# Counting one port for GpSimd and VectorE in the model that writes a fused attention, gated product and expert kernel's order

## The chip, the cores and the metric

The kernel runs on one core of a Trainium2 chip. The metric is the device time of one execution in microseconds (us). Five engines work side by side, each through its own queue and strictly in that queue's order: TensorE (PE; its weight loads are shown apart, as PEld), VectorE (DVE), ScalarE (ACT), GpSimd (POOL) and SyncE (SP), which here only issues DMA transfers. An engine waits for another through semaphores, where the data demand it.

## The reference

Three steps follow one another: attention in chunks with eight memory keys, a gated product, and eight experts whose weights are balanced over all 3072 tokens before they are used.

```python
for c in range(nc):                       # chunks of 32 queries, of 16 + 32 + 8 keys and 8 memory keys
    scores = scale * np.matmul(q_c, k_full.transpose(0, 1, 3, 2))
    a = np.exp(scores - np.max(scores, axis=-1, keepdims=True))
    a = a / (np.sum(a, axis=-1, keepdims=True) + 1e-09)
    out[:, :, c_start:c_end] = np.matmul(a, v_full)
...
x = (x @ w_a) * (x @ w_b) @ w_out         # 3072 x 512, through 1536
...
P = np.exp(x @ w_gate - max)              # 3072 x 8, then scaled over rows and columns 8 times
for e in range(8):
    out += P[:, e:e + 1] * (np.maximum(x @ w1[e], 0.0) @ w2[e])   # 512 -> 1024 -> 512
```

## The kernel before, in words

Every matrix factor is split into a high part (its fp32r rounding, made by ACT) and a low part (the factor less its high part, made by DVE or POOL), and each product is three matmuls.

The first part, up to some 820 us, holds attention and the gated product. Attention goes by 64 groups of 96 queries and four heads: scores on PE (`s_ps`, L401); mask and scale on DVE (`masked`, L410, reading PSUM and one tile in SBUF); the row maximum on DVE (L416); four exponentials on ACT (L419); a tiny addition and a reciprocal of the sums on DVE (`sm`, L425 and L428); the scaling by them on POOL (`norm`, `s_sb`, L431); transposes on PE (`t_ps`, L438), a copy on ACT, the values on PE (`o_ps`, L448), and the high and low part of the result (L456 on ACT, L459 on DVE). The weights of the gated product come in six pieces of 128x512 for each of 24 weight steps. In the first six steps a piece is first turned from 64-bit to 32-bit numbers: L215 on ACT, then `d_clamp` L219, `d_shift` L223, `d_top` L230 and `d_low` L237 on DVE, in the tiles `raw_e` and `raw_m`. In all steps ACT then makes the high part of a piece (L251) and POOL the low one (`w_low`, L255, called a low below). The products are `pab` on PE (12 matmuls a product), `a_sb` on DVE (L549, reads PSUM), `gh` on ACT (L555), its low part `gl` on DVE (L558, two tiles in SBUF), `po` on PE and its sum `acc` on DVE (L573, reads PSUM). From 210 us on DVE and ACT also prepare weights of the experts ahead (tiles `dbuf` and `pbuf`, L271 and L287).

The second part multiplies the experts by a scheme with seven instead of eight block products (`pa`, `px` for the first product, `py`, `pr` for the second). DVE adds, subtracts and splits 128x1024 tiles (`hb`, `xbig`, L271), and `settle` (L928) multiplies by the gate: `hb<-part,pb` with two operands in SBUF, `hb<-pa,pb` with one in PSUM. Until about 1200 us POOL makes the low parts of the experts' weights (`wbig<-raw_e`, 28 of 128x768 and 28 of 128x1024); behind that it has nothing more to do.

The order in each engine's queue is set when the program is built. `Order.add(engine, cost, due, f, *after)` notes an operation, its cost in us, its due number and what it follows. `Order.emit` plays a clock through these costs: whenever an engine is free in the model, it takes the ready operation with the smallest due, and the instructions are written out in that order. There is one `Order` for each part. The model's times go nowhere else: on the chip only the queues' orders and the semaphores are left. In `emit` the engines are visited in the order in which they first occur in the list of operations, DVE ahead of POOL in both parts.

Of the kernel before, what the change touches and what calls it, by code (L numbers as in the profile page):

```python
# [15 lines left out]
ALU = mybir.AluOpType  # L16
# [30 lines left out]
class Order:  # L47

# [10 lines left out]
    def add(self, engine, cost, due, f, *after):  # L59
        self.ops.append((engine, cost, due, f, [x for x in after if x is not None]))  # L60
        return len(self.ops) - 1

    def emit(self):
        follow = [[] for _ in self.ops]
        missing = [len(op[4]) for op in self.ops]
        for x, op in enumerate(self.ops):
            for y in op[4]:
                follow[y].append(x)
        BEGIN, FREE, DONE = range(3)
        ready = {op[0]: [] for op in self.ops}  # L70
        busy = dict.fromkeys(ready, False)

        events = [(0.0, x, BEGIN) for x, m in enumerate(missing) if m == 0]
        heapq.heapify(events)
        begin = [0.0] * len(self.ops)
        left = len(self.ops)
        while events:
            now = events[0][0]
            while events and events[0][0] <= now:
                _, x, what = heapq.heappop(events)  # L80
                engine, cost, due, f, after = self.ops[x]
# [10 lines left out]
            for engine, queue in ready.items():  # L92
                if queue and not busy[engine]:
                    _, x = heapq.heappop(queue)
                    cost, f, store = self.ops[x][1], self.ops[x][3], engine == "ACT" and self.ops[x][1] == 0.1
                    busy[engine] = True
                    f()
                    left -= 1
                    heapq.heappush(events, (now + cost, x, FREE))
                    land = self.land if engine == "SP" or store else 0.0  # L100
                    heapq.heappush(events, (now + cost + land, x, DONE))
        assert left == 0
# [3 lines left out]
def tile_kernel(ctx: ExitStack, tc, qT, kw, vw, w_moe, w_gate, w_ex, out):  # L106
# [166 lines left out]
    def weight_ops(add, w, blocks, sums, due, loaded, before=(), pool=True):  # L273
# [5 lines left out]
        y = add("DVE", 0.42, d, lambda: sub(s1, w22, w21, ALU.add), loaded, *before)  # L279
        y = add("DVE", 0.42, d, lambda: sub(s3, w11, w21), y)  # L280
        y = add("DVE", 0.42, d, lambda: sub(s2, s1, w11), y)
        summed = add("DVE", 0.42, d, lambda: sub(s4, w12, s2), y)
        done = []
        for cost, x, a, n, y in ((0.83, 0, blocks, 3, loaded), (1.05, 3, sums, 4, summed)):
            h, lo = w[:, x:x + n, 0, :], w[:, x:x + n, 1, :]
            a = a[:, :n * Q].rearrange("p (i n) -> p i n", i=n)
            y = add("ACT", cost, d, lambda h=h, a=a: nc.scalar.activation(out=h, in_=a, func=AF.Copy), y, *before)  # L287
            done.append(y)
            if pool:
                done.append(add("POOL", 2.4 * cost, d, lambda h=h, lo=lo, a=a: sub(lo, a, f32(h), engine=nc.gpsimd), y))  # L290
                continue
            for b in range(0, n, 2):
                c = min(b + 2, n)
                done.append(add(
                    "DVE", 0.35 * (c - b), d, lambda h=h[:, b:c], lo=lo[:, b:c], a=a[:, b:c]: sub(lo, a, f32(h)), y))
        return done

    def token_ops(add, sb, due, stage, cs, after, free, ahead=1.0, gate=()):
# [16 lines left out]
        def split(i, src, d, *deps):  # L315
            h, lo = (x[:, i, cs[0]:cs[0] + n].rearrange("p c t -> p (c t)") for x in x7)
            y = add("ACT", 1.05 * k1, d, lambda: nc.scalar.activation(out=h, in_=src, func=AF.Copy), *deps, free[i], *gate)
            return add("DVE", 1.2 * k1, d, lambda: sub(lo, src, f32(h)), y)
# [3 lines left out]
        y1 = add("DVE", 1.2 * k1, due, lambda: sub(n0, b22, b12), in22, in12, *gate)  # L322
        y2 = add("DVE", 1.2 * k1, due, lambda: sub(b12, b12, b11), y1, in11)
        y3 = add("DVE", 1.2 * k1, due, lambda: sub(n1, b22, b12), y2)
# [5 lines left out]
        y4 = add("DVE", 1.2 * k1, due + 0.05, lambda: sub(b11, b21, n1), y3, ready[B11])  # L330
# [6 lines left out]
    with ExitStack() as pa:  # L337
# [53 lines left out]
        def attn_group(x, i, g, qk_loaded, v_loaded, due):  # L391
# [72 lines left out]
            y = add("DVE", 0.07, due, sums, *[add("ACT", 0.39, due, lambda j=j: exps(j), y) for j in range(4)])  # L464
# [62 lines left out]
        def moe_step(x, n, s, k):  # L527
# [63 lines left out]
            for f in range(NF):  # L591
# [13 lines left out]
                z = add("DVE", 0.47, due, lambda f=f: g_low(f), z)  # L605
# [357 lines left out]
    def operands(g):  # L963
# [5 lines left out]
        for k, (q, j) in enumerate(((0, 0), (0, 1), (1, 0), (1, 1))):  # L969
            done = [h_done[g, q, j, i] for i in range(2)]  # L970
            if g < HOLD:
# [3 lines left out]
                    "DVE", 1.2, at - 0.1 + 0.2 * q, lambda src=src, dst=dst, j=j:  # L975
# [10 lines left out]
        def split(p, src, n, *deps):  # L986
# [6 lines left out]
            y = add("DVE", 1.2, d, lambda: sub(lo, src, f32(h)), y)  # L993
# [4 lines left out]
        def summed(o, a, b, n, *deps):  # L998
            return add("DVE", 1.2, at + (n - 2.2) * step, lambda: sub(o, a, b), *deps)
# [247 lines left out]
```

## Time and profile before

| | |
|---|---|
| three runs | 2684.62, 2686.83, 2687.25 us (median 2686.83) |
| the profiled execution | 2686.72 us, of which the span of the instructions is 2684.7 us |
| PE busy in the span | 2620.5 us (98%) |
| DVE busy | 2141.1 us (80%) |
| ACT busy | 1056.2 us (39%) |
| POOL busy | 458.8 us (17%), 270 instructions |

Times inside the profile count from the span's start. Busy time is the time in which an instruction of the engine was running or held at its start; an instruction that is ready but held therefore shows as one that takes long. PE's busy time also holds matmuls that wait in its pipeline, so it says little about a full PE. The chain of waits follows the work that ended last back to the start: each piece of it is a time that nothing else covered.

### The profile page before, as it was taken

Reading aid. Unit: us, or ns where it says so; the run is one execution under the profiler, and the core shown is the slowest. Engines: PE = TensorE matmul, PEld = TensorE weight load, DVE = VectorE, ACT = ScalarE, POOL = GpSimd, SP = SyncE. Lnnn points to the kernel's source line nnn. Section 1 sums busy time; section 2 is a strip of 40 time slices with the busy share of each in tenths; the row PEclk is TensorE's granted clock in tenths of the full one; section 3 lists DMA queues with packets and bytes.
Section 4 is the critical chain, followed back from the end, with each engine's and each line's share of the span. In section 5 each row is a group of like instructions: output and inputs, shape, how many; then the busy total and the mean of one; then the engine's idle time right before and its main releaser. Section 6 shows DMA issues by size and latency. Waiting matters only on the chain.

```text
span 2684.7 us, 36063 instructions
## 1 busy us (share of the span) xinstructions
PE 2620.5 (98%) x13147; PEld 2240.8 (83%) x13147; DVE 2141.1 (80%) x3091; ACT 1056.2 (39%) x1914; POOL 458.8 (17%) x270
## 2 busy tenths in 40 slices
PE   6989999999999999999999999999999999999998
PEld 4879989989997788888887888888888888888887
DVE  8994787787768899989999587777789587777777
ACT  6643554654434433433333332222324322222222
POOL 4433342343311422322220000000000000000000
PEclk8999999999999999999999999999999999999999
DMA  7653677777835666666676766666666766666663
GB/s 231 200 162 113 236 247 269 253 245 277 288 108 181 216 231 235 211 246 217 228 257 204 220 202 199 202 203 191 202 219 212 217 198 205 198 194 203 199 187 112
DMA packets 224079, 565.05 MB, mean 210 GB/s; under 512 B 21232, under 2 KB 41712, under 8 KB 219808
## 3 DMA queue, kind: packets, MB, share of 16 engines
q1 hardware_dynamic: 190112, 445.31, 52.8%
q10 hardware_dynamic: 33792, 117.44, 11.6%
q8 instruction: 105, 1.72, 0.3%
q14 instruction: 70, 0.57, 0.1%
HBM read 423.12 MB, written 139.56 MB: 210 GB/s over the span
## 4 chain that ended last, share of the span: by engine, by line
PE 90%; DVE 7%; issue 1%; POOL 1%; ACT 1%; DMA 0%; SPq 0%; ACTq 0%; POOLq 0%; DVEq 0%
PE py L262 25%; PE pa L262 19%; PE pab L262 14%; PE px L262 14%; PE po L262 7%; PE pr L262 7%; PE s_ps L401 1%; DVE sums L271 1%; DVE xbig L271 1%; PE o_ps L448 1%; PE t_ps L438 1%; PE pl L583 1%; DVE hb L271 1%; POOL s_sb L431 1%; DVE gl L558 1%
## 5 line engine op out<-in xcount | busy, mean ns | idle before, releaser
L262 PE MATMUL py<-xbig,wbig 128*128 128x512 f32 x3168 | 801.7, 390 | 4.8 <-DVE sums L271 2.9
L262 PEld LDWEIGHTS py<-xbig,wbig 128*128 128x128 f32 x3168 | 592.3, 188 | 136.8 <-DVE sums L271 10.5
L992 ACT ACTIVATE xbig<-hb 128x1024 fp32r<-128x1024 f32 x336 | 354.9, 1061 | 671.0 <-PE py L262 471.0
L262 PE MATMUL pa<-xbig,wbig 128*128 128x512 f32 x2304 | 586.4, 390 | 1.9 <-DVE part L271 1.3
L271 DVE TENSOR_TENSOR xbig<-hb,xbig 128x1024 fp32r<-128x1024 f32 x336 | 433.9, 1293 | 106.8 <-ACT xbig L992 106.6
L262 PEld LDWEIGHTS pa<-xbig,wbig 128*128 128x128 f32 x2304 | 431.1, 188 | 92.9 <-DVE part L271 2.5
L271 DVE TENSOR_TENSOR sums<-py,sums 128x512 f32<-128x512 f32 x495 | 339.1, 686 | 156.8 <-PE py L262 152.3
L262 PE MATMUL pab<-xbig,wbig 128*128 128x384 f32 x2304 | 448.2, 343 | 0.7 <-ACT a_sb L546 0.7
L262 PE MATMUL px<-xbig,wbig 128*128 128x512 f32 x1728 | 441.6, 390 | 1.0 <-DVE part L271 0.6
L262 PEld LDWEIGHTS pab<-xbig,wbig 128*128 128x128 f32 x2304 | 410.2, 192 | 6.1 <-ACT a_sb L546 0.9
L262 PEld LDWEIGHTS px<-xbig,wbig 128*128 128x128 f32 x1728 | 322.9, 188 | 68.7 <-DVE part L271 1.4
L271 POOL TENSOR_TENSOR wbig<-raw_e,wbig 128x768 fp32r<-128x768 f32 (+1 forms) x56 | 172.0, 3072 | 447.4 <-ACT wbig L287 367.3
L271 DVE TENSOR_TENSOR hb<-hb,hb 128x1024 f32<-128x1024 f32 x192 | 234.8, 1231 | 1.0
L262 PE MATMUL po<-gh,wbig 128*128 128x384 f32 x768 | 234.0, 346 | 0.0
L914 ACT ACTIVATE part<-pa 128x512 f32<-128x512 f32 x192 | 114.3, 595 | 289.7 <-PE pa L262 288.9
L262 PE MATMUL pr<-xbig,wbig 128*128 128x512 f32 x864 | 217.2, 389 | 0.4 <-DVE sums L271 0.4
L928 DVE SCALAR_TENSOR_TENSOR hb<-part,pb 128x512 f32<-128x512 f32 x276 | 193.6, 705 | 2.8
L262 PEld LDWEIGHTS pr<-xbig,wbig 128*128 128x128 f32 x864 | 162.1, 188 | 34.2 <-DVE sums L271 0.6
L271 DVE TENSOR_TENSOR part<-px,part 128x512 f32<-128x512 f32 x192 | 131.6, 686 | 36.7 <-PE px L262 34.7
L573 DVE TENSOR_TENSOR acc<-po,acc 128x384 f32<-128x384 f32 x160 | 88.3, 552 | 75.2 <-PE po L262 74.6
L262 PEld LDWEIGHTS po<-gh,wbig 128*128 128x128 f32 x768 | 143.4, 190 | 5.8
L255 POOL TENSOR_TENSOR wbig<-raw_e,wbig 128x512 fp32r<-128x512 f32 x96 | 127.5, 1348 | 87.1 <-ACT wbig L251 86.9
(121 smaller groups left out, 2219.3 us busy)
## 6 DMA issues: line engine op xcount, KB each, us to landing
wbig<-wc SPq DMA_DIRECT2D x336, 512.0 KB, 3.8
wbig<-wc SPq DMA_DIRECT2D x476, 256.0 KB, 3.3
wc<-xbig ACTq DMA_DIRECT2D x36, 1792.0 KB, 7.7
wc<-wbig ACTq DMA_DIRECT2D x28, 1792.0 KB, 8.3
raw_e<-w_f SPq DMA_DIRECT2D x72, 256.0 KB, 5.0
raw_e<-in_w_ex SPq DMA_DIRECT2D x28, 512.0 KB, 5.3
pb<-pT SPq DMA_DIRECT2D x23, 512.0 KB, 4.9
dbuf<-in_w_moe SPq DMA_DIRECT2D x18, 512.0 KB, 4.6
```

Of the source, the lines that this page charges most:

```text
L255: nc.gpsimd.tensor_tensor(out=wl, in0=raw(part), in1=f32(wh), op=ALU.subtract)
L262: nc.tensor.matmul(out=out, lhsT=a, rhs=b, start=first and i + j == 0, stop=last and i == n - 1 and j == 2, skip_group_check=skip,)
L271: (engine or nc.vector).tensor_tensor(out=out, in0=a, in1=b, op=op)
L401: nc.tensor.matmul(out=s_banks[:TQ, j % 2, 2 * g + j // 2, :], lhsT=qps[i % NQ][a:a + 64, (h0 + j) // 2, :], rhs=kts[i][a:a + 64, (h0 + j) ...
L431: nc.gpsimd.tensor_tensor(out=r["s"], in0=r["s"], in1=r["sm"][:, :, None].to_broadcast([TQ, 4, TK]), op=ALU.mult)
L438: nc.tensor.transpose(r["t_ps"][:, j, :], r["s"][:, j, :], ident[:TQ, :TQ])
L448: nc.tensor.matmul(out=r["o_ps"][a:a + 64, j // 2, :], lhsT=vts[i][:, h0 + j, :], rhs=r["pt"][:, 2 * (j % 2) + j // 2, :], start=True, sto ...
L558: nc.vector.tensor_tensor(out=r["gl"][:, f, :], in0=r["a", f], in1=f32(r["gh"][:, f, :]), op=ALU.subtract)
L573: nc.vector.tensor_tensor(out=a, in0=r["o", d], in1=a, op=ALU.add)
L914: "ACT", 0.6, at + 0.05, lambda: nc.scalar.activation(out=parts[j], in_=src, func=AF.Copy),
L928: y = add("DVE", 0.69, due, lambda: nc.vector.scalar_tensor_tensor(out=dst, in0=src, scalar=0.0, in1=pb[:, j * HB:(j + 1) * HB], op0=ALU.m ...
L992: "ACT", 1.05, d, lambda: nc.scalar.activation(out=h, in_=src, func=AF.Copy), *deps, *t_used.get(t_n - NTR, ()))
```

## The change

The model gets one more resource, a port. Operations on POOL, and those on DVE that are now noted as "DVE+", take it while they run, one at a time; while it is taken, DVE may still start an operation that is noted as "DVE". Each engine has two lists of ready operations, and takes the smaller due of the two, or of the one that it may use. Costs, dues and dependencies stay as they were, and no semaphore, tile or instruction is added or taken away. "DVE+" are the sums and splits on SBUF, `sm` (L425), the four conversion steps and `gl`; `masked`, the maxima, the reciprocals, whatever reads PSUM, and `settle` stay "DVE".

```diff
     def add(self, engine, cost, due, f, *after):
-        self.ops.append((engine, cost, due, f, [x for x in after if x is not None]))
+        port = engine in ("DVE+", "POOL")
+        self.ops.append((engine.rstrip("+"), cost, due, f, [x for x in after if x is not None], port))
...
-        ready = {op[0]: [] for op in self.ops}
+        ready = {op[0]: ([], []) for op in self.ops}
         busy = dict.fromkeys(ready, False)
+        port = False
...
                 if what == FREE:
                     busy[engine] = False
+                    port = port and not ported
                 elif what == BEGIN:
-                    heapq.heappush(ready[engine], (due, x))
+                    heapq.heappush(ready[engine][ported], (due, x))
...
+            for engine, queues in ready.items():
+                if busy[engine]:
+                    continue
+                queues = [q for ported, q in enumerate(queues) if q and not (ported and port)]
+                if not queues:
+                    continue
+                _, x = heapq.heappop(min(queues, key=lambda q: q[0]))
+                cost, f, ported, store = self.ops[x][1], self.ops[x][3], self.ops[x][5], engine == "ACT" and self.ops[x][1] == 0.1
+                busy[engine] = True
+                port = port or ported
...
-            y = add("DVE", 0.07, due, sums, *[add("ACT", 0.39, due, lambda j=j: exps(j), y) for j in range(4)])
+            y = add("DVE+", 0.07, due, sums, *[add("ACT", 0.39, due, lambda j=j: exps(j), y) for j in range(4)])
...
                     for cost, f in ((0.34, d_clamp), (0.34, d_shift), (0.6, d_top), (0.6, d_low)):
-                        y = add("DVE", cost, due, lambda f=f, p=p: f(i, p), y)
+                        y = add("DVE+", cost, due, lambda f=f, p=p: f(i, p), y)
...
-                z = add("DVE", 0.47, due, lambda f=f: g_low(f), z)
+                z = add("DVE+", 0.47, due, lambda f=f: g_low(f), z)
```

The lines of the functions move down by five. DVE's queue has 3026 rows (rows of equal instructions counted once) before; it differs from the new one between row 27 and row 1853, POOL's between row 10 and 106 of 176, PE's between row 16 and 1840 of 2736. Three places follow, each before and after.

The first is on DVE in the first stage, around the first `raw_m` row (the first conversion step of a weight piece); `sm` and `nm` are sums and maxima of an attention group. Before:

```order
L428 RECIPROCAL sm<-sm 96x4
L237 SCALAR_TENSOR_TENSOR raw_e<-pbuf,raw_e 128x512
L459 TENSOR_TENSOR xbig<-o_ps,xbig 128x2x96
L416 TENSOR_REDUCE nm<-s_sb 96x4
L219 TENSOR_SCALAR raw_m<-raw_m 128x512
L410 SCALAR_TENSOR_TENSOR s_sb<-s_ps,abuf 96x512
L223 TENSOR_SCALAR raw_m<-raw_m 128x512
L416 TENSOR_REDUCE nm<-s_sb 96x4
L230 SCALAR_TENSOR_TENSOR raw_m<-dbuf,raw_m 128x512
```

The same place after:

```order
L430 TENSOR_SCALAR sm<-sm 96x4
L224 TENSOR_SCALAR raw_m<-raw_m 128x512
L242 SCALAR_TENSOR_TENSOR raw_e<-pbuf,raw_e 128x512
L433 RECIPROCAL sm<-sm 96x4
L421 TENSOR_REDUCE nm<-s_sb 96x4
L415 SCALAR_TENSOR_TENSOR s_sb<-s_ps,abuf 96x512
L464 TENSOR_TENSOR xbig<-o_ps,xbig 128x2x96
L421 TENSOR_REDUCE nm<-s_sb 96x4
L228 TENSOR_SCALAR raw_m<-raw_m 128x512
```

The reciprocal, which lets POOL begin a `norm`, now has four rows behind it that the model lets run beside POOL; before, `raw_m` rows stood between such rows.

The second is on POOL, right behind a run of twelve low parts without a `norm` between them; `wbig` rows are low parts of weights, `s_sb` rows are `norm`. Before:

```order
L255 TENSOR_TENSOR wbig<-raw_m,wbig 128x512 x2
L431 TENSOR_TENSOR s_sb<-s_sb,sm 96x512
L255 TENSOR_TENSOR wbig<-raw_e,wbig 128x512
L431 TENSOR_TENSOR s_sb<-s_sb,sm 96x512
L255 TENSOR_TENSOR wbig<-raw_e,wbig 128x512 x3
L431 TENSOR_TENSOR s_sb<-s_sb,sm 96x512 x2
L255 TENSOR_TENSOR wbig<-raw_m,wbig 128x512 x2
L431 TENSOR_TENSOR s_sb<-s_sb,sm 96x512
```

After:

```order
L260 TENSOR_TENSOR wbig<-raw_m,wbig 128x512 x2
L436 TENSOR_TENSOR s_sb<-s_sb,sm 96x512 x2
L260 TENSOR_TENSOR wbig<-raw_e,wbig 128x512 x4
L436 TENSOR_TENSOR s_sb<-s_sb,sm 96x512 x2
L260 TENSOR_TENSOR wbig<-raw_m,wbig 128x512 x2
L436 TENSOR_TENSOR s_sb<-s_sb,sm 96x512
```

The four low parts of `raw_e` now stand together. Over the first part POOL's queue holds five runs of exactly four low parts before, and eight after.

The third is on DVE a little later, between two `gl` of the gated product; `dbuf` and `xbig<-dbuf` rows are preparation of the experts' weights. Before:

```order
L558 TENSOR_TENSOR gl<-a_sb,gh 128x384
L271 TENSOR_TENSOR dbuf<-dbuf 128x256
L410 SCALAR_TENSOR_TENSOR s_sb<-s_ps,abuf 96x512
L271 TENSOR_TENSOR dbuf<-dbuf 128x256
L416 TENSOR_REDUCE nm<-s_sb 96x4
L271 TENSOR_TENSOR dbuf<-dbuf 128x256
L549 TENSOR_TENSOR a_sb<-pab,a_sb 128x384
L271 TENSOR_TENSOR dbuf<-dbuf 128x256
L271 TENSOR_TENSOR xbig<-dbuf,xbig 128x2x256
```

After:

```order
L563 TENSOR_TENSOR gl<-a_sb,gh 128x384
L415 SCALAR_TENSOR_TENSOR s_sb<-s_ps,abuf 96x512
L421 TENSOR_REDUCE nm<-s_sb 96x4
L554 TENSOR_TENSOR a_sb<-pab,a_sb 128x384
L276 TENSOR_TENSOR dbuf<-dbuf 128x256 x2
L430 TENSOR_SCALAR sm<-sm 96x4
L433 RECIPROCAL sm<-sm 96x4
L563 TENSOR_TENSOR gl<-a_sb,gh 128x384
```

Rows on two tiles in SBUF and rows that the model lets run beside POOL took turns one by one; now they stand in runs of one kind.

## Rows read from the trace of the kernel before

**Rows 1.** Busy time by stage: us of each engine (instructions), clock, DMA

```profile
0.00:210.00 210.00, 172.19 (x1171) 149.93 (x1172) 187.01 (x360) 126.85 (x410) 83.48 (x69) 0.90 0.63 197
350.00:630.00 280.00, 269.85 (x1777) 250.32 (x1776) 220.63 (x416) 155.41 (x411) 107.37 (x76) 0.99 0.74 255
820.00:1500.00 680.00, 673.36 (x2983) 549.42 (x2982) 613.95 (x795) 268.06 (x340) 171.98 (x56) 1.00 0.65 224
1500.00:2685.00 1185.00, 1175.47 (x5205) 970.41 (x5203) 908.91 (x1141) 363.00 (x445) 0.00 (x0) 1.00 0.64 197
```

**Rows 2.** Timeline from 25 us, DVE and POOL: start, us taken

```profile
25.42 0.42 DVE L219 TENSOR_SCALAR raw_e<-raw_e 128x512 f32<-128x512 f32 x1
...
26.42 2.22 DVE L219 TENSOR_SCALAR raw_e<-raw_e 128x512 f32<-128x512 f32 x1
...
26.09 1.04 POOL L431 TENSOR_TENSOR s_sb<-s_sb,sm 96x512 f32<-96x512 f32 x1 [4.07 <-ACT raw_e L215]
27.09 1.27 POOL L255 TENSOR_TENSOR wbig<-raw_e,wbig 128x512 fp32r<-128x512 f32 x1
```

**Rows 3.** Groups by shape, DVE, 0 to 210 us: busy, mean ns, idle

```profile
L223 DVE TENSOR_SCALAR raw_e<-raw_e 128x512 int32<-128x512 int32 x24 | 15.7, 657 | 0.1
L219 DVE TENSOR_SCALAR raw_e<-raw_e 128x512 f32<-128x512 f32 x24 | 14.7, 613 | 0.5 <-ACT raw_e L215 0.5
L219 DVE TENSOR_SCALAR raw_m<-raw_m 128x512 f32<-128x512 f32 x12 | 12.9, 1079 | 0.0
L425 DVE TENSOR_SCALAR sm<-sm 96x4 f32<-96x4 f32 x29 | 12.6, 434 | 1.0 <-ACT s_sb L419 1.0
...
L428 DVE RECIPROCAL sm<-sm 96x4 f32<-96x4 f32 x29 | 4.8, 165 | 0.2
```

**Rows 4.** Chain of waits, 0 to 210 us: start, us, what

```profile
26.50 2.15 DVE raw_e L219
...
159.17 5.97 DVE raw_m L219
...
193.88 2.12 POOL s_sb L431
```

**Rows 5.** Chain of waits, 350 to 630 us

```profile
358.93 2.50 DVE gl L558
...
368.12 2.85 POOL s_sb L431
...
619.69 4.18 DVE gl L558
```

**Rows 6.** Timeline from 351 us, DVE, POOL and PE; idle before in brackets

```profile
351.35 0.55 DVE L558 TENSOR_TENSOR gl<-a_sb,gh 128x384 fp32r<-128x384 f32 x1
...
357.70 5.00 POOL L255 TENSOR_TENSOR wbig<-raw_e,wbig 128x512 fp32r<-128x512 f32 x4
...
358.85 4.28 DVE L558 TENSOR_TENSOR gl<-a_sb,gh 128x384 fp32r<-128x384 f32 x1
...
363.18 0.44 PE L262 MATMUL po<-gl,wbig 128*128 128x384 f32 x1 [0.90 <-DVE gl L558]
```

**Rows 7.** Groups by shape, DVE, 350 to 630 us

```profile
L558 DVE TENSOR_TENSOR gl<-a_sb,gh 128x384 fp32r<-128x384 f32 x35 | 37.9, 1084 | 0.3
...
L271 DVE TENSOR_TENSOR pbuf<-pbuf 128x256 f32<-128x256 f32 x40 | 28.7, 746 | 0.0
```

**Rows 8.** Timeline from 864 us, POOL and DVE

```profile
864.17 23.08 POOL L271 TENSOR_TENSOR wbig<-raw_e,wbig 128x768 fp32r<-128x768 f32 x2 [9.44 <-ACT wbig L287]
...
882.72 2.27 DVE L271 TENSOR_TENSOR hb<-hb,hb 128x1024 f32<-128x1024 f32 x1
884.91 2.88 DVE L928 SCALAR_TENSOR_TENSOR hb<-part,pb 128x512 f32<-128x512 f32 x1
```

**Rows 9.** Groups by shape, DVE, 820 to 1500 us

```profile
L928 DVE SCALAR_TENSOR_TENSOR hb<-part,pb 128x512 f32<-128x512 f32 x96 | 70.9, 741 | 1.0
...
L928 DVE SCALAR_TENSOR_TENSOR hb<-pa,pb 128x512 f32<-128x512 f32 x32 | 21.8, 683 | 0.3 <-PE pa L262 0.3
```

More of the change, by code (lines that the diff above doesn't have):

```diff
@@ L80, in emit @@
                 _, x, what = heapq.heappop(events)
-                engine, cost, due, f, after = self.ops[x]
+                engine, cost, due, f, after, ported = self.ops[x]
                 if what == FREE:
                     busy[engine] = False
+                    port = port and not ported
                 elif what == BEGIN:
-                    heapq.heappush(ready[engine], (due, x))
+                    heapq.heappush(ready[engine][ported], (due, x))
                 else:
@@ L91, in emit @@
                             heapq.heappush(events, (now + hop, y, BEGIN))
[L92 to L101, printed above, removed]
+            for engine, queues in ready.items():
[8 more added lines that the diff above has]
+                port = port or ported
+                f()
+                left -= 1
+                heapq.heappush(events, (now + cost, x, FREE))
+                land = self.land if engine == "SP" or store else 0.0
+                heapq.heappush(events, (now + cost + land, x, DONE))
         assert left == 0
@@ L278, in weight_ops @@
         d = due
[L279 to L282, printed above, removed]
+        y = add("DVE+", 0.42, d, lambda: sub(s1, w22, w21, ALU.add), loaded, *before)
+        y = add("DVE+", 0.42, d, lambda: sub(s3, w11, w21), y)
+        y = add("DVE+", 0.42, d, lambda: sub(s2, s1, w11), y)
+        summed = add("DVE+", 0.42, d, lambda: sub(s4, w12, s2), y)
         done = []
@@ L294, in weight_ops @@
                 done.append(add(
-                    "DVE", 0.35 * (c - b), d, lambda h=h[:, b:c], lo=lo[:, b:c], a=a[:, b:c]: sub(lo, a, f32(h)), y))
+                    "DVE+", 0.35 * (c - b), d, lambda h=h[:, b:c], lo=lo[:, b:c], a=a[:, b:c]: sub(lo, a, f32(h)), y))
         return done
@@ L317, in split @@
             y = add("ACT", 1.05 * k1, d, lambda: nc.scalar.activation(out=h, in_=src, func=AF.Copy), *deps, free[i], *gate)
[L318 removed]
+            return add("DVE+", 1.2 * k1, d, lambda: sub(lo, src, f32(h)), y)
         ready = [None] * 7
         ready[B11] = split(B11, b11, due, in11)
[L322 to L324 removed]
+        y1 = add("DVE+", 1.2 * k1, due, lambda: sub(n0, b22, b12), in22, in12, *gate)
+        y2 = add("DVE+", 1.2 * k1, due, lambda: sub(b12, b12, b11), y1, in11)
+        y3 = add("DVE+", 1.2 * k1, due, lambda: sub(n1, b22, b12), y2)
         ready[B21] = split(B21, b21, due + 0.01, in21)
@@ L329, in token_ops @@
         ready[B22] = split(B22, b22, due + 0.05, in22)
-        y4 = add("DVE", 1.2 * k1, due + 0.05, lambda: sub(b11, b21, n1), y3, ready[B11])
+        y4 = add("DVE+", 1.2 * k1, due + 0.05, lambda: sub(b11, b21, n1), y3, ready[B11])
         ready[T4] = split(T4, b11, due + 0.06, y4)
@@ L974, in operands @@
                 done = [add(
-                    "DVE", 1.2, at - 0.1 + 0.2 * q, lambda src=src, dst=dst, j=j:
+                    "DVE+", 1.2, at - 0.1 + 0.2 * q, lambda src=src, dst=dst, j=j:
                     nc_mult(nc.vector, dst, src, pb[:, None, j * HB:(j + 1) * HB].to_broadcast([P, 2, HB])),
@@ L992, in split @@
                 "ACT", 1.05, d, lambda: nc.scalar.activation(out=h, in_=src, func=AF.Copy), *deps, *t_used.get(t_n - NTR, ()))
-            y = add("DVE", 1.2, d, lambda: sub(lo, src, f32(h)), y)
+            y = add("DVE+", 1.2, d, lambda: sub(lo, src, f32(h)), y)
             out[p] = t_n, y
@@ L998, in summed @@
         def summed(o, a, b, n, *deps):
-            return add("DVE", 1.2, at + (n - 2.2) * step, lambda: sub(o, a, b), *deps)
+            return add("DVE+", 1.2, at + (n - 2.2) * step, lambda: sub(o, a, b), *deps)
         d11, d12, d21, d22 = ready[0, 0], ready[0, 1], ready[1, 0], ready[1, 1]
```

1 line of the change is left out of this document (removed).

## The prediction

> **What bounds the kernel now.** I read the busy time by stage first [rows 1], to see where PE can be helped at all. From 1500 us on POOL does nothing, and there the change cannot touch anything but the place where it starts: the model's port is then taken by DVE alone, which runs one operation at a time anyway. From 820 to 1500 us PE issues 2983 matmuls in 680 us, 4.387 per us; from 1500 us on it issues 5205 in 1185 us, 4.392 per us. The two rates differ by 0.1%, so in the second part PE is full although POOL works beside it, and DVE, at 614 of 680 us, just keeps up. The first part is another matter: from 0 to 210 us DVE is busy for 187 of 210 us and PE issues few matmuls at a granted clock of 0.90; from 350 to 630 us DVE is busy for 221 of 280.
>
> Next, what DVE's busy time is made of. The timeline shows L219 at 25.42 us taking 0.42 us while POOL is idle, and the same instruction on another piece at 26.42 taking 2.22 us; POOL ran a `norm` from 26.09 and a low from 27.09 to 28.36 [rows 2]. DVE's instruction ended 0.3 us behind POOL's second one: it did not slip in between the two but stood until POOL had nothing more. At 864 us it is the other way round: two of POOL's instructions take 23.08 us, as long as DVE ran one sum or split on SBUF straight behind another; once DVE had run a sum that reads PSUM, its next one took 2.27 us instead of some 1.2 and POOL got through [rows 8]. So the two do exclude each other, for whole instructions, and the one that holds the port keeps it as long as it has work queued without a gap. The groups by shape give the size: from 0 to 210 us `sm` takes 434 ns on average, where the reciprocal on the same tile takes 165; L219 on `raw_m` 1079 ns against 420 unheld, L219 on `raw_e` 613, L223 657 [rows 2, 3].
>
> Last, the chain of waits, since only held time on the chain costs anything. From 0 to 210 us I find ten pieces on it that are far longer than the instruction alone: the first at 26.50 us, the longest 5.97 us at 159.17, the last at 193.88 [rows 4]; seven are DVE's (L219 three times, L223 once, `sm` three times), three are `norm` on POOL. Together they are 26.2 us. From 350 to 630 us there are six: four `gl` and two `norm`, 19.1 us together [rows 5].
>
> **The change part by part.** No instruction, wait or transfer is added; only rows change places. PE's queue stays nearly the same: a group's transposes or values stand one product later or earlier. So the whole effect is which rows of DVE stand beside which of POOL, and all of it lies in held time. The transfers on SP's queue move with their due numbers by a few rows, and nothing on the chain waits for one behind the first tiles, so I cost them at nothing; if a piece of weights came late, the conversion behind it would be, and DVE with it.
>
> Term one, 0 to 210 us. The ten pieces, 26.2 us, less what they would take unheld: four conversion steps at 0.42, three `sm` at 0.17 (the reciprocal's time, the nearest row) and three `norm` at 1.04 are 5.3 us [rows 2, 3]. That leaves 20.9 us that the chain lost to the port. The same from DVE's side, whatever is on the chain: 29 x 0.27 for `sm`, 12 x 0.66 and 24 x 0.19 for L219, 24 x 0.24 for L223 are 26.0 us. So a perfect order is worth 21 to 26 us here, none at all is worth 0. The first place shown of DVE's queue says that the order goes the right way: behind the reciprocal, which releases a `norm`, stand four rows that need no port, worth some 2 us, as long as POOL's `norm` and a low (1.04 and 1.27 us). I take half, 10.4 us. Not all, because nothing on the chip makes the two engines meet as they do in the model: a `norm` is tied to DVE by its reciprocal, but a low starts when ACT has made its high part, and half of the seven DVE pieces stood behind lows. What is late next in their place is DVE itself, which even without held time has some 160 us of work in this stage.
>
> Term two, 350 to 630 us. Six pieces, 19.1 us, less four `gl` at 0.55 and two `norm` at 1.04 leave 14.8 us. The timeline shows what a long `gl` is: POOL ran four lows in one go for 5.00 us from 357.70, `gl` came at 358.85 and took 4.28 us, and PE stood for it at 363.18 [rows 6]. In the model the port is free at the end of each low, and DVE, which is visited first, would take it there; the chip let POOL run through. So the model expects such a `gl` to cost at most one low, and the order does not avoid the case. The `norm` pieces, where DVE's rows held POOL, and the runs on `dbuf` and `pbuf` (746 ns on average for `pbuf` [rows 7]) are what it can better. I take a third of 14.8, 4.9 us; the bounds are 14.8 and, by the first rival, a loss.
>
> Term three, the second part. PE is full there; what DVE gains or loses is hidden behind 680 us of matmuls as long as DVE has idle time, 66 us now [rows 1]. I take 0.
>
> One kind of instruction speaks against the model. `settle` from `part` has two operands in SBUF and is not counted as taking the port, so the new order puts it where POOL runs. At 884.91 us one took 2.88 us while POOL was at work, and in 820 to 1500 us it takes 741 ns on average against 683 for the one that reads PSUM: 96 x 0.058, 5.6 us held now, all hidden [rows 8, 9]. By the Trainium skill, GPSIMD Engine Reference, section Key points, GpSimd contends with VectorE instructions "in a 2-port perf mode or with two SBUF inputs"; by that rule every such `settle` beside POOL is held, and the trace agrees with the one at 884.91. By the row the sum stays at 0 here, since present holds of other rows go away in exchange; by the rule alone it would be the third rival below.
>
> The sum is made against the profiled execution: 2686.7 us, 2684.7 of them the span, 0.1 us under the median of the runs. 2686.7 - 10.4 - 4.9 = 2671.4, so 2671 us, 0.6% faster. A measurement of this kernel tells about 0.2%, 5.4 us, from no change.
>
> **The rivals.**
> First, slower: POOL's lows run in longer trains. The new queue of POOL has eight runs of four lows where the old one had five; the second place shown joins one low and three to four. Behind a run of four a `gl` lost 4.28 - 0.55 = 3.7 us, and a `norm` that stands behind the run comes 3.8 us later (three lows more at 1.27). If the three new runs each catch a `gl` and the first stage gains nothing because its lows too come in trains, the time is 2686.7 + 3 x 3.7 = 2698. It decides from three such pieces on, since they take back the 10.4 us of term one. For it speaks that the chip demonstrably does not hand over between POOL's instructions [rows 2, 6]; against it that POOL often waited for ACT's high parts, which breaks a train.
>
> Second, no change: held time goes from one row to the next but the chain finds as much of it, because what the model calls simultaneous isn't. Then 2682 to 2692 us.
>
> Third, slower by `settle`: if each of POOL's 56 instructions [rows 1] held one of them for 2.2 us (2.88 - 0.69), that would be 123 us of DVE time, more than its 66 us of idle time; PE would lose the rest, 57 us. It decides from 30 of 56 on; with 40 held the loss is 22 us and the time 2709. Against it: 96 of them lose 5.6 us in all today.
>
> Fourth, more gain: all held pieces leave the chain, 2686.7 - 20.9 - 14.8 = 2651, or 2646 with DVE's own 26.0 for the first stage.
>
> **How the numbers follow.** The forecast (2660 to 2681) gets 0.45, the fourth rival 0.14, no change 0.17, the first rival 0.20, the third 0.04. Faster is 0.59, the same 0.17, slower 0.24. The range goes from 2642, under the fourth rival, to 2699, over the first; only the third lies outside, and what is left to mechanisms that I have not seen.
>
> **What would show it.** From 0 to 210 us, `sm` and L219 on `raw_m` should average nearer 0.3 and 0.75 us than 0.43 and 1.08, and POOL's `norm` should lie beside rows that read PSUM; the product that ends at 210 us should end some 10 us sooner. From 350 to 630 us I expect one or two of the four long `gl` to be left or more, and `dbuf` and `pbuf` rows nearer 0.41 us. If the mean of `gl` rises above 1.08 us and five or more long pieces of it are on the chain, the first rival is right. If PE's matmuls from 820 to 1500 us come at less than 4.39 per us, the third. The prediction is wrong above all if the first stage, where DVE is nearly full, gains nothing.

## The result and the profile after

The changed kernel takes 2656.72 us (median; 2655.03 to 2659.55) against 2685.72 us before in the same session: ratio 0.9894, interval 0.9876 to 0.9911. It is 1.1% faster, 29 us where 15 were forecast: inside the whole range (2642 to 2699), but below the forecast's own 2660 to 2681. The profiled execution takes 2657.31 us with a span of 2655.5.

To see where the 29 us come from I cut both traces at the same work: at the start of the 174th, 404th, 807th and last (1152nd) matmul of `po`, and of the 1109th of `py`. In the old order these lie at 206.7, 357.3, 630.6, 809.0 and 1516.7 us, the first four close to the borders that the prediction used. Two more columns say what PE lost in each stretch, before and after: its waits (idle time of 0.1 us or more ahead of an instruction), and the loss to the clock, the stretch's length times the share by which the granted clock was below full.

| stretch | before, us | after, us | difference | PE's waits | lost to the clock |
|---|---|---|---|---|---|
| to the 174th `po` | 206.7 | 186.8 | -19.9 | 37.7, 21.8 | 20.5, 15.4 |
| to the 404th | 150.6 | 146.1 | -4.5 | 0.0, 0.0 | 3.4, 0.0 |
| to the 807th | 273.3 | 262.2 | -11.1 | 10.1, 0.9 | 3.4, 1.7 |
| to the 1152nd | 178.4 | 179.8 | +1.4 | 0.0, 0.1 | 0.0, 3.4 |
| to the 1109th `py` | 707.7 | 712.6 | +4.9 | 6.8, 11.4 | 0.0, 1.7 |
| the rest | 1168.0 | 1168.1 | +0.1 | 3.8, 3.8 | 1.8, 0.5 |

The two losses account for the differences to within some 2 us a stretch. The first part ends 34.2 us sooner: PE waits 25 us less in it (47.8 before, 22.9 after) and loses 7 us less to the clock (27.3 and 20.5).

The same stretches as windows, columns as in [rows 1]:

```profile
0.00:187.00 187.00, 165.19 (x1150) 145.52 (x1150) 161.38 (x345) 124.02 (x399) 82.98 (x68) 0.92 0.67 210
333.00:595.00 262.00, 261.07 (x1740) 244.21 (x1739) 206.67 (x405) 151.54 (x400) 100.98 (x75) 0.99 0.76 266
786.00:1471.00 685.00, 673.52 (x2983) 551.51 (x2983) 623.86 (x796) 266.93 (x340) 149.62 (x56) 1.00 0.64 222
1471.00:2650.00 1179.00, 1175.10 (x5204) 970.39 (x5202) 908.51 (x1140) 361.55 (x443) 0.00 (x0) 1.00 0.64 197
```

From 786 to 1471 us PE issues the 2983 matmuls in 685 us that took it 680 before, 4.355 per us instead of 4.387; behind that the rate is the old one.

What lies behind the two big differences is read best from what PE waited for in the first part, first before, then after (us in total, times, longest):

```profile
PE t_ps L438 <- POOL s_sb L431: 17.2, 11, 2.2
PE po L262 <- DVE gl L558: 9.5, 6, 3.8
PE s_ps L401 <- DVE s_sb L410: 8.7, 5, 3.1
```

```profile
PE t_ps L443 <- POOL s_sb L436: 6.5, 4, 2.3
PE s_ps L406 <- DMA abuf<-in_kw: 6.2, 2, 4.8
PE s_ps L406 <- DVE s_sb L415: 4.2, 4, 1.4
```

The transposes now wait for `norm` four times instead of eleven, and the wait of `po` for `gl` is gone: the longest `gl` of the first part takes 1.66 us, where four took over 4.2. Groups by shape on DVE, 0 to 190 us, which answer to [rows 3] (29 of `sm` in both):

```profile
L228 DVE TENSOR_SCALAR raw_e<-raw_e 128x512 int32<-128x512 int32 x23 | 14.5, 636 | 0.0
...
L224 DVE TENSOR_SCALAR raw_e<-raw_e 128x512 f32<-128x512 f32 x24 | 9.7, 413 | 0.0
L430 DVE TENSOR_SCALAR sm<-sm 96x4 f32<-96x4 f32 x29 | 9.7, 337 | 0.0
...
L224 DVE TENSOR_SCALAR raw_m<-raw_m 128x512 f32<-128x512 f32 x10 | 4.8, 479 | 0.0
```

The first conversion step on `raw_m` fell from 1079 to 479 ns, on `raw_e` from 613 to 413 ns, which is its unheld time; `sm` from 434 to 337. And from 320 to 600 us, beside [rows 7]:

```profile
L276 DVE TENSOR_TENSOR pbuf<-pbuf 128x256 f32<-128x256 f32 x44 | 30.3, 691 | 0.0
...
L563 DVE TENSOR_TENSOR gl<-a_sb,gh 128x384 fp32r<-128x384 f32 x35 | 25.3, 722 | 1.5 <-ACT gh L560 1.4
```

`gl` fell from 1084 to 722 ns; `pbuf`, which nothing on the way waits for, hardly moved. I call an instruction's time above the tenth percentile of its shape its held time (differences under 0.03 us left out). Summed over DVE it is 40.6 us before and 20.6 after in the first stretch; in the third, `gl` alone has 18.9 and 6.1.

The second part shows the opposite, 786 to 1471 us, beside [rows 9]:

```profile
L933 DVE SCALAR_TENSOR_TENSOR hb<-part,pb 128x512 f32<-128x512 f32 x96 | 116.8, 1219 | 0.8
...
L933 DVE SCALAR_TENSOR_TENSOR hb<-pa,pb 128x512 f32<-128x512 f32 x32 | 21.7, 679 | 0.0
```

`settle` from `part` is held for half a microsecond each time: 96 x (1.219 - 0.679) = 52 us of DVE, nine times the 5.6 us of before. That is the hold that the prediction's third rival named. Other rows gave most of it back, as the prediction said; two of them, first before (820 to 1500 us), then after:

```profile
L271 DVE TENSOR_TENSOR xbig<-hb,xbig 128x1024 fp32r<-128x1024 f32 x118 | 167.7, 1425 | 20.2 <-ACT xbig L992 20.2
...
L271 DVE TENSOR_TENSOR raw_e<-raw_e 128x256 f32<-128x256 f32 x112 | 80.4, 720 | 0.8 <-DMA raw_e<-in_w_ex 0.8
```

```profile
L276 DVE TENSOR_TENSOR xbig<-hb,xbig 128x1024 fp32r<-128x1024 f32 x118 | 152.4, 1294 | 5.3 <-ACT xbig L997 5.3
...
L276 DVE TENSOR_TENSOR raw_e<-raw_e 128x256 f32<-128x256 f32 x112 | 62.1, 555 | 12.1 <-DMA raw_e<-in_w_ex 12.1
```

They take 33.6 us less, and DVE's busy time rose by 10 us only, from 614 of 680 to 624 of 685 us.

### The profile page after: what moved, and what is told of

Its sections match the earlier page's. It is cut to its first block, busy times and chain, and to the rows that moved or that the text cites. A ratio compares the mean times of both kernels' runs of the same rounds, so it can differ in the third digit from the quotient of the medians.

```text
span 2655.5 us, 36040 instructions
## 1 busy us (share of the span) xinstructions
PE 2611.6 (98%) x13147; PEld 2237.3 (84%) x13147; DVE 2118.5 (80%) x3091; ACT 1053.6 (40%) x1914; POOL 431.8 (16%) x270
## 4 chain that ended last, share of the span: by engine, by line
PE 66%; DVE 6%; DMA 1%; issue 1%; ACT 0%; SPq 0%; ACTq 0%; DVEq 0%
PE py L267 23%; PE pa L267 17%; PE px L267 14%; PE pr L267 7%; PE pab L267 3%; PE po L267 2%; DVE xbig L276 2%; DVE sums L276 1%; DMA raw_e<-in_w_ex 1%; DVE hb L933 1%; DVE raw_e L276 1%; DVE hb L276 1%; DVE part L276 0%; PE py L1118 0%; ACT xbig L997 0%
## 5 line engine op out<-in xcount | busy, mean ns | idle before, releaser
L276 DVE TENSOR_TENSOR xbig<-hb,xbig 128x1024 fp32r<-128x1024 f32 x336 | 418.7, 1247 | 91.4 <-ACT xbig L997 91.1
L267 PE MATMUL pab<-xbig,wbig 128*128 128x384 f32 x2304 | 441.0, 339 | 0.1
L267 PEld LDWEIGHTS pab<-xbig,wbig 128*128 128x128 f32 x2304 | 403.6, 190 | 5.3 <-DVE a_sb L554 0.5
L933 DVE SCALAR_TENSOR_TENSOR hb<-part,pb 128x512 f32<-128x512 f32 x276 | 239.5, 871 | 2.6
L276 POOL TENSOR_TENSOR wbig<-raw_e,wbig 128x768 fp32r<-128x768 f32 (+1 forms) x56 | 149.6, 2672 | 473.3 <-ACT wbig L292 377.8
L260 POOL TENSOR_TENSOR wbig<-raw_e,wbig 128x512 fp32r<-128x512 f32 x96 | 133.8, 1415 | 61.2 <-ACT wbig L256 49.0
```

The source lines that it names most:

```text
L260: nc.gpsimd.tensor_tensor(out=wl, in0=raw(part), in1=f32(wh), op=ALU.subtract)
L267: nc.tensor.matmul(out=out, lhsT=a, rhs=b, start=first and i + j == 0, stop=last and i == n - 1 and j == 2, skip_group_check=skip,)
L276: (engine or nc.vector).tensor_tensor(out=out, in0=a, in1=b, op=op)
L933: y = add("DVE", 0.69, due, lambda: nc.vector.scalar_tensor_tensor(out=dst, in0=src, scalar=0.0, in1=pb[:, j * HB:(j + 1) * HB], op0=ALU.m ...
```

## The experiments

My theory, A: the gain is held time that left the way of PE, and the loss in the second part is `settle`. Rival B: the new order is a better sequence of the groups, port or not. Rival C: the second part cannot take up what the first gains, whatever its order.

**One Order at a time.** The model counts the port in one of the two Orders alone; an Order without it makes the order of before.

```diff
-    def __init__(self, land):
+    def __init__(self, land, ports=True):
+        self.ports = ports
...
-        port = engine in ("DVE+", "POOL")
+        port = self.ports and engine in ("DVE+", "POOL")
...
-    order = Order(7.0)
+    order = Order(7.0, ports=False)
```

> The model counts the port in the first Order alone; the second part's order is made as before. Theory A (the first part's gain of 34 us is held time that left the chain; the 5 us given back from 820 us on come from the second part's own new order, in which settle from part is held): the 34 us stay and nothing is given back, about 2652 us, ratio 0.987 to before. Rival C (the second part waits for something that does not come earlier, whatever its order): the 5 us are given back all the same, about 2657 us as with the whole change.

> The model counts the port in the second Order alone. Theory A: the first part takes what it took before, the second loses some 5 us to held settle rows, about 2691 us, ratio 1.002; settle from part takes about 1.2 us on average against 0.74 before. Rival C: nothing is lost where nothing came early, 2686 us, ratio 1.000.

The first part alone: 2657.81 us, ratio 0.9895 (0.9882 to 0.9909), the whole change again. The second alone: 2687.69 us, 1.0008 (1.0000 to 1.0017). So the gain lies in the first part, and the second part's new order costs at most 0.17%. The 2652 us that A expected of the first did not come. Its profiled execution, the slowest of the four (2660.16 us), can't decide between A and C by its time: in the third stretch it needed 268.0 us, the changed kernel 262.2 in the very same order. The stretch to the 1109th `py`, with the old order, took 708.5 us, 0.8 more than before, so C's rule does not hold there. First its wait on PE from 370 to 420 us and two windows (columns as in [rows 1]), then the same of the changed kernel:

```profile
PE o_ps L454 <- ACT pt L448: 2.4, 1, 2.4
```

```profile
380.00:390.00 10.00, 8.54 (x62) 7.67 (x61) 5.04 (x11) 4.47 (x9) 2.40 (x4) 1.00 0.92 303
390.00:400.00 10.00, 9.07 (x41) 8.85 (x42) 7.00 (x17) 5.18 (x16) 2.55 (x3) 0.66 0.66 251
```

```profile
PE o_ps L453 <- ACT pt L447: 0.9, 1, 0.9
```

```profile
380.00:390.00 10.00, 9.07 (x71) 8.09 (x69) 6.38 (x14) 5.36 (x10) 3.60 (x3) 1.00 0.92 307
390.00:400.00 10.00, 10.00 (x62) 9.72 (x64) 9.29 (x18) 6.71 (x18) 5.30 (x5) 1.00 0.84 290
```

PE had stood still for 2.4 us (0.9 in the other run), waiting for a copy on ACT, and then the granted clock was 0.66 for 10 us: part of them ran at the lower of the clock's two levels, 1.2 instead of 2.4 GHz: 41 matmuls instead of 62. One order thus varies by some 6 us from run to run, and the length of a stretch in one profile is read to no better than that. PE's waits vary less: 2.4 us in this stretch here, 0.9 with the change, 10.1 before.

**`settle` counted.**

```diff
-                y = add("DVE", 0.69, due, lambda: nc.vector.scalar_tensor_tensor(
+                y = add("DVE" if src is A else "DVE+", 0.69, due, lambda: nc.vector.scalar_tensor_tensor(
```

> As the change, but settle from part, with two operands in SBUF, is also noted as DVE+. Theory A: settle from part goes back to about 0.75 us on average, other rows are held instead, and the 5 us lost in the second part mostly come back: 2652 us (2649 to 2655). Rival C: 2657 us as with the whole change. A third way: with more rows taking the port the model starts settle later, and the tiles it writes come later: 2660 us or more.

2655.22 us, 0.9883 (0.9868 to 0.9898). DVE's rows of `settle` from `part` in this kernel and, below it, in second_part_only, 786 to 1519 us:

```profile
L933 DVE SCALAR_TENSOR_TENSOR hb<-part,pb 128x512 f32<-128x512 f32 x102 | 70.4, 704 | 0.2
```

```profile
L934 DVE SCALAR_TENSOR_TENSOR hb<-part,pb 128x512 f32<-128x512 f32 x97 | 100.7, 1040 | 0.9
```

The hold is gone, but the stretch to the 1109th `py` still takes 710.9 us. A's account of the second part falls in part: `settle`'s held time is not what costs there. But the new order itself does cost: PE's waits in this stretch are 8.7 to 11.4 us in all six profiles with a new second order, this one included, and 6.2 to 6.8 in all eight with the old one.

**The marks turned round.** `masked`, the maxima, the reciprocals and the PSUM readers take the model's port, the rows that the chip holds do not.

```diff
-            taken[x] = y = add("DVE", 0.6, due, masked, scored[x], turned.get(x - 4))
+            taken[x] = y = add("DVE+", 0.6, due, masked, scored[x], turned.get(x - 4))
...
-                z = add("DVE+", 0.47, due, lambda f=f: g_low(f), z)
+                z = add("DVE", 0.47, due, lambda f=f: g_low(f), z)
```

> In the first Order the marks are turned round: masked, the maxima, the reciprocals and every row that reads PSUM take the port in the model, while the sums and splits on SBUF, sm, the conversion steps and gl do not; the second Order counts no port. Theory A (what counts is that rows which the chip holds stay away from POOL's): the rows that the chip holds now stand beside POOL's on purpose, nothing is gained in the first part and probably 10 to 30 us are lost, 2690 to 2715 us, sm over 0.43 us on average from 0 to 210 us. Rival B (any order that takes DVE's rows apart in this way, or another sequence of the attention groups, gains): as much as with the port in the first part alone, about 2652 us.

2687.22 us (eleven runs, 2684.40 to 2696.76), 1.0013 (1.0002 to 1.0024): no gain, against B, but hardly a loss either, against A's number. The stretches say more: the first takes 213.0 us (6.3 more), the third 261.6 (11.7 less), although DVE's held time there rose from 40.9 to 49.9 us:

```profile
L277 DVE TENSOR_TENSOR pbuf<-pbuf 128x256 f32<-128x256 f32 x40 | 35.8, 927 | 0.0
...
L564 DVE TENSOR_TENSOR gl<-a_sb,gh 128x384 fp32r<-128x384 f32 x34 | 23.9, 706 | 6.0 <-ACT gh L561 5.9
```

It is `gl` that counts: 706 ns here too, by chance of the order (one long `gl` of 3.76 us is left, and two more stand outside this stretch), while `pbuf` is held more than before or with the change at no cost. Held time as a sum says nothing in this stretch.

**One kind of row at a time.** conv_only counts `sm` and the conversion steps alone on DVE, gl_only counts `gl` alone; both with the old order in the second part.

> In the first Order the port is counted for norm and the low parts on POOL and, on DVE, for sm and the four conversion steps alone; gl and the preparation rows are plain DVE; no port in the second Order. Theory A: the first stage ends some 20 us sooner, as with all rows counted, and the stretch that lay between 357 and 631 us before keeps its 273 us, since gl stays held: about 2666 us, ratio 0.992. Rival B (the sequence as a whole gains, not which rows are counted): the gain is not split by stage, anything between 2650 and 2686 us.

> As before, but on DVE gl alone is counted. Theory A: the first stage stays near 206 us, the stretch of 273 us (357 to 631 us before) takes some 262 us because gl's held time falls from 18.9 us to 6 or less, while the preparation rows on dbuf and pbuf may be held longer at no cost: about 2675 us, ratio 0.996. Rival B: no gain in that stretch, or gain without a fall of gl's held time; 2686 us or any other.

conv_only: 2679.28 us, 0.9970 (0.9960 to 0.9980); gl_only: 2671.58 us, 0.9947 (0.9934 to 0.9960). The third stretch went as expected: 271.8 us with `gl` held for 19.0 us, 265.4 with 6.6. The first did not: 198.2 and 199.1 us, some 8 us gained by either instead of 20 and 0. In conv_only the conversion's held time did halve (30.4 to 15.9 us), but other rows were held longer. POOL's `norm` and DVE's `gl` to 198 us:

```profile
L437 POOL TENSOR_TENSOR s_sb<-s_sb,sm 96x512 f32<-96x512 f32 x29 | 43.8, 1516 | 71.6 <-DVE sm L434 46.4 <-PE po L268 5.6 <-ACT acc L577 5.4
```

```profile
L564 DVE TENSOR_TENSOR gl<-a_sb,gh 128x384 fp32r<-128x384 f32 x16 | 14.9, 933 | 0.0
```

`norm` took 1342 ns before, 1303 with the change, 1516 here; `gl` 666 ns before and 609 with the change (0 to 210 and 0 to 190 us), 933 here. That these rows ate what conv_only lacks to 20 us is likely, not shown: the two gains add up to 16 of the 19.9 us, and both profiles are the slowest of their runs (2681.32 of 2671.19 to 2681.32; 2675.54 of 2671.04 to 2675.54). In PE's waits of this stretch conv_only gains 9.8 us, gl_only 4.3, the change 15.9.

**The low parts left out.**

```diff
-                lows[i, p] = add("POOL", 1.23, due, lambda p=p: w_low(i, p), highs[i, p], *used)
+                lows[i, p] = add("POOL-", 1.23, due, lambda p=p: w_low(i, p), highs[i, p], *used)
```

"POOL-" is on POOL and takes no port in the model. In this order, as in keeps_first and keeps_settle below, two loads change places and one 64-bit piece of weights is overwritten before it is converted; the instructions stay the same.

> In the first Order all of the change's DVE rows and norm take the port, the low parts on POOL do not; no port in the second Order. The step of the prediction by which half of the first stage's held time could not be avoided (a low starts when ACT is done, so the order can't steer it): if that step is right, leaving the lows out loses nothing, the first stage ends 18 to 20 us sooner all the same and gl is held as with the whole change: about 2657 us. If the lows can be steered: the first stage gains 10 us or less and the long gl rows behind four lows come back: 2670 to 2680 us.

2665.16 us, 0.9928 (0.9915 to 0.9941), between the two. The first stretch takes 190.3 us: 16.3 of the 19.9 us come without counting a single low part. Counting them is worth some 8 us of the whole, 2665 against 2657; two `gl` take 4.05 us again in the third stretch, where `gl` is held for 10.9 us. Long `gl` rows separate the orders at full size: where `gl` and the lows are both counted (the change, first_part_only, settle_counted, gl_only and the last three below), no `gl` takes over 2.4 us; where not both are, three or four take 3.7 to 5.0 us.

**POOL made short.** POOL's two operations of the first part work on a small piece, in the old and in the new order.

```diff
-        nc.gpsimd.tensor_tensor(out=wl, in0=raw(part), in1=f32(wh), op=ALU.subtract)
+        nc.gpsimd.tensor_tensor(out=wl[:, :8], in0=raw(part)[:, :8], in1=f32(wh)[:, :8], op=ALU.subtract)
...
-                    out=r["s"], in0=r["s"], in1=r["sm"][:, :, None].to_broadcast([TQ, 4, TK]), op=ALU.mult
+                    out=r["s"][:, :, :2], in0=r["s"][:, :, :2], in1=r["sm"][:, :, None].to_broadcast([TQ, 4, 2]), op=ALU.mult
```

> The order of before; POOL's two operations of the first part work on a small piece only (low parts on 8 of 512 columns, norm on 2 of 128 keys of each head), so POOL holds the port for a short time; the rest of the low parts stays zero and most of the attention weights stay unscaled. POOL fills the low parts with zeros once at the start. Theory A: what the port costs in the old order goes away, and some of norm's own time on the chain with it: the first stage 25 to 45 us shorter, the stretch of 273 us at 255 to 262, altogether 2625 to 2650 us. Rival B (the port costs little, the new order gains by its sequence): 2670 to 2680 us, by norm's own time alone.

> The changed order, with POOL's two operations of the first part cut to the same small pieces as in the short run of the old order (low parts on 8 of 512 columns, norm on 2 of 128 keys of each head; the rest stays zero or unscaled). Theory A (the change gains by keeping held rows apart and by nothing else): with hardly anything left to hold, the new order is worth nothing over the old one: 2640 to 2650 us, beside 2644 for the old order. Rival B (a better sequence of the groups, port or not): it is still some 25 us ahead, 2615 to 2625 us.

Old order: 2644.07 us, 0.9849 (0.9836 to 0.9863). New order: 2656.27 us, 0.9890 (0.9873 to 0.9906). In the old one DVE's first conversion step is at its unheld time and POOL's operations are short (before, they took 1.3 us):

```profile
L219 DVE TENSOR_SCALAR raw_e<-raw_e 128x512 f32<-128x512 f32 x24 | 9.9, 413 | 0.2 <-ACT raw_e L215 0.2
```

```profile
L431 POOL TENSOR_TENSOR s_sb<-s_sb,sm 96x8 f32<-96x8 f32 x64 | 32.0, 500 | 291.8 <-DVE sm L428 200.4 <-ACT wbig L251 39.6 <-ACT gh L555 23.4
L255 POOL TENSOR_TENSOR wbig<-raw_e,wbig 128x8 fp32r<-128x8 f32 x96 | 26.7, 279 | 158.4 <-ACT wbig L251 157.9
```

This settles B. With next to nothing left to hold, the old order gains 41 us and the new one none (2656.27 beside 2656.72 at full size): as a sequence it is not better but some 11 us worse (6.6 us in the profiles). The gain of the change hangs on the time for which POOL's operations last.

Short operations also empty POOL's queue sooner, so a second reading is left: that `norm` waits less behind lows in the new order. The profiles at full size speak against it. In the first stretch the 29 `norm` began 18.6 us in total behind their reciprocals, where it was 8.0 before, and took 37.8 us against 38.9. Rows kept apart are what remains.

**POOL runs through in the model.** The engine that had the port last is visited first.

```diff
-            for engine, queues in ready.items():
+            for engine, queues in sorted(ready.items(), key=lambda e: e[0] != holder):
...
                 port = port or ported
+                holder = engine if ported else holder
```

> The port is counted in the first Order alone, as in first_part_only, but the engine that had the port last is visited first when it is free again, so that in the model POOL runs through its queue as it did on the chip (5.00 us for four low parts in one go). If the model's error at that place costs something: gl and the conversion steps are held for less than 20.6 and 6 us, and the first part ends 3 to 10 us sooner than with the port alone: 2645 to 2655 us. If not (the chip's times drift from the model's anyway): 2655 to 2660 us, as first_part_only. If long trains become more frequent because the model no longer breaks them: over 2665 us.

> As keeps_first, in both Orders, and with settle from part noted as DVE+. Theory A: the first part as in keeps_first, and the second part loses 3 us or less with settle from part at 0.75 us or less on average: 2643 to 2655 us, the best of all; if the model's rule at that place is worth nothing: 2655 us as with settle_counted.

> As keeps_settle, with one more edit: the room in dbuf and pbuf into which a 64-bit piece of weights is loaded is now picked when the operation is listed, not when it is written out. In lows_not_counted, keeps_first and keeps_settle two loads change places, and one piece in pbuf is overwritten before its conversion has read it, which changes some weights of the gated product, but no instruction and no wait of another kind. If those times may be read as times of their orders, as assumed: 2651 us as keeps_settle (2648 to 2655), ratio 0.9866, and the first part ends 35 to 40 us sooner than in the old order. If the swapped load was what made it faster: 2656 us or more.

The last one's further edit:

```diff
-        doubles[s, part] = rooms[len(doubles) % ND]
+        doubles[s, part] = rooms[n % ND]
...
-                    y = add("SP", 0.5, due - EARLY, lambda p=p: d_load(i, p), *merged[:len(merged) - ND + 1][-1:])
+                    y = add("SP", 0.5, due - EARLY, lambda p=p, n=len(merged): d_load(i, p, n), *merged[:len(merged) - ND + 1][-1:])
```

keeps_first: 2655.51 us, 0.9881 (0.9866 to 0.9895), hardly better than the port alone (2657.81). keeps_settle: 2651.52 us, 0.9866 (0.9852 to 0.9881). keeps_rooms: 2649.27 us (2648.33 to 2654.44), 0.9875 (0.9858 to 0.9891), so the swapped load was not what made it faster. In keeps_rooms `gl` is at 615 ns and `pbuf` at 464 from 332 to 594 us, 722 and 691 with the change. The first part ends 39.7 us sooner than in the old order, against 34.2 for the change. The eight runs of the last two, 2648.3 to 2654.4 us, all lie below the four of the change, but the intervals of the ratios overlap: probably some 5 us better, not settled. Nor is it shown that the rule for POOL does it: the order of the first part is the same in all three, PE waits 22.8 to 23.1 us in it against 22.9 with the change, and the lead of the last two there is the clock, which cost 15.4 us against 20.5 in keeps_first and in the change.

## Why the prediction came out as it did

**The mechanism** was right: the two engines shut each other out, only held time on PE's way costs, and the order alone can move it. Wrong was the rule that the one that holds the port keeps it as long as it has work queued; the last section counts it. Two of the three terms were sized too low. The chain of waits after the change breaks off at 651 us, so its pieces can't be counted against [rows 4, 5]; PE's waits and the stretches stand in.

**Term one** was forecast at 10.4 us and measured at 19.9 (20.4 and 23.0 in the two other profiles of the same order); 15.9 us of it are PE's waits. The bound fits (20.9 by the chain; 27.7 with POOL made short, which also shortens `norm` itself), the half did not. The step that failed is the reason given for the half: a low starts when ACT is done, so the pieces behind lows can't be steered. All seven pieces of DVE on the chain, not half of them, stood behind a `norm` with lows in its train. A `norm` is released by DVE's own reciprocal, so rows that need no port behind the reciprocal keep DVE clear of `norm` and of the low behind it. lows_not_counted bears it out: 16.3 us without steering the lows.

**Term two** was forecast at 4.9 us and measured at 11.1 (5.3 and 12.3 in the two other profiles of the same order), of 15.7 with POOL made short. In PE's waits the gain is 9.2 us (7.7 and 8.7 in the other two). The step that failed: "the order does not avoid the case" of `gl` behind four lows. POOL still runs four in a row, but `gl` gets in between them. Timeline after, from 332 us:

```profile
332.74 5.56 POOL L260 TENSOR_TENSOR wbig<-raw_e,wbig 128x512 fp32r<-128x512 f32 x4
...
334.39 1.34 DVE L563 TENSOR_TENSOR gl<-a_sb,gh 128x384 fp32r<-128x384 f32 x1
335.66 1.49 DVE L276 TENSOR_TENSOR dbuf<-dbuf 128x256 f32<-128x256 f32 x1
```

`gl` ended at 335.73 and a `dbuf` row at 337.15, while POOL's four lows lasted until 338.30; in [rows 6] `gl` stood until all four were through. I had also expected the gain from `norm`, `dbuf` and `pbuf`; it was `gl`, as gl_only shows (265.4 us). `pbuf` stayed at 691 ns and `dbuf` at 528 instead of nearing 410.

**Not foreseen**: 4.5 us between the two stretches. PE waits for nothing there, before or after; 3.4 us of it are the clock. Before, the granted clock fell to its lower level behind two rows of 24 short matmuls (`pl`, the experts' gate), and the next product took 3.89 and 3.75 us; after, it took 2.33 us behind both. The first of the two, before, then after:

```profile
261.58 2.74 PE L583 MATMUL pl<-gate,acc 128*128 128x8 f32 x24
264.18 3.89 PE L262 MATMUL pab<-xbig,wbig 128*128 128x384 f32 x12
```

```profile
240.39 2.74 PE L588 MATMUL pl<-gate,acc 128*128 128x8 f32 x24
242.99 2.33 PE L267 MATMUL pab<-xbig,wbig 128*128 128x384 f32 x12
```

The order does not decide it: settle_counted and first_part_only, with the same order there, have both falls and gain 1.4 us. About 3 of the 4.5 us are luck.

**Term three** was 0 and the profile lost 4.9 us. The hold of `settle` came: 741 ns rose to 1219, and fell to 704 once it was counted. The Trainium skill (GPSIMD Engine Reference, section Key points) names contention of GpSimd with VectorE instructions that have two SBUF inputs, and the trace agrees with it. But the hold cost little: other rows were held less, and DVE was idle for 61 of 685 us even so. The sign that the prediction had named for that rival, fewer than 4.39 matmuls per us, came all the same, and not mainly through it: settle_counted has no such hold, and its stretch is 1.7 us shorter. The step that failed is that PE is full there and everything on DVE hidden: in the new order PE waits for 11.4 us in all against 6.8, most of it for DVE's `sums`, `part` and `xbig` rows. In the runs the loss is smaller, 0.08% in second_part_only.

In the other twelve orders this stretch loses 0.8 to 3.8 us against before, also with the old second order (0.8 to 3.3; 2.3 to 3.8 with the new). With the old one PE waits as before, and the clock makes the difference: 0.8 to 0.9 us in the three profiles in which it cost nothing there, as before, and 2.2 to 3.3 in the four in which it cost 1.7 to 3.4. What the last 0.9 us are stays open. Rival C falls with this: two of these three, first_part_only and lows_not_counted, had gained 27.5 and 24.9 us in the first part and kept all but 0.9.

**The rivals.** Longer trains (2698) did not come: the new runs of four lows catch no `gl` for longer than 1.66 us. No change, too, is out; the hold on `settle` was there, its price (2709) was not. Held time that leaves PE's way altogether (2651) came closest to the 2656.7 measured. The forecast (2671) had the gain at half its size, and that the clock gave 7 us of it in the first part was in no term.

## What to carry to other kernels

A list scheduler that knows two engines to shut each other out can move their meetings to rows that nobody waits for; what it is worth is read from the waits of the engine that bounds, not from the sum of held time (in other_rows the sum rose and the stretch got shorter). Mark all rows that the two engines hold against each other: a part of them gained a part (8 us each of 20 in the first stretch). To see whether an order gains as a sequence or by what it avoids, shrink the thing avoided and time both orders again.

## What the runs showed of the hardware

I counted, instruction by instruction, the cases of the first part in which a DVE row stood held (0.15 us or more) when POOL began its next instruction, less than 0.1 us behind its last. Two counts for each kind of passage, DVE ran in between / POOL ran on:

```
                 norm, low   low, low   low, norm   norm, norm
before             0 / 14    26 / 22      2 / 0        -
after              1 / 3     36 / 2         -         4 / 0
```

So POOL does not simply keep the port, as I had thought from [rows 2, 6]. Behind a `norm` with a low in its train DVE almost never got in; between two lows mostly: in 59 of 62 cases in which it had come 0.41 to 1.27 us ahead of the low's end and had not been passed before. Of the rows that had come less than 0.3 us ahead none got in; the four long `gl` of the old order are among them (0.13 to 0.15 us), and were passed three times each. What decides was not tried by itself. Of POOL's own time, the short pieces show how little is fixed in a low: 279 ns on 8 columns against some 1.3 us on 512. Of a `norm` more is: 500 ns on 8 columns against 1.04 us on 512.
